# A new written-out order for a sketched attention with an MLP: loads on two queues, batch-0 queries loaded by head pairs

## The chip, the core and the metric

The kernel runs on one core of a Trainium2 chip. The core has five engines that work side by side, each with its own queue of instructions in a fixed order: TensorE (PE, matmuls; its weight loads are listed as PEld), VectorE (DVE), ScalarE (ACT), GpSimd (POOL) and SyncE (SP, which here only issues DMAs). An instruction that waits holds back everything behind it on its engine. The metric is the device time of one execution in microseconds (us), median of three runs.

## The reference

Two blocks follow each other. The first is an attention with a polynomial sketch, for batch 4, heads 4, sequence 1088 and head size 32, with r = 8:

```
a = S1 x,  b = S2 x                      # 8 numbers each, for x = q and x = k
phi(x) = a outer b                       # 64 features per token
kv = sum over tokens of phi(k) v         # 64 x 32 per head
z  = sum over tokens of phi(k)           # 64 per head
attn = phi(q) kv / (phi(q) z + 1e-6)
```

The heads are then laid side by side to rows x of 128 numbers, and the second block is

```
xn  = (x - mean) / sqrt(var + 1e-6) * g
out = x + relu(xn w_ch1) w_ch2           # w_ch1 128 x 512, w_ch2 512 x 128
```

q, k, v and g are float32; S1, S2, w_ch1 and w_ch2 are float64 and are turned into float32 on the chip with integer and float steps on their two 32-bit words.

## The kernel before, in words

All work is written as small named operations, and one long string, PROGRAM (from line 851), lists them in the order in which they are issued; an operation's first argument is often the engine (S SyncE, A ScalarE, V VectorE, G GpSimd). Each engine's queue is that list, filtered to the engine. No scheduler changes it.

For a batch b, the steps are: load k (ld, 544 KB, all 1088 tokens; batch 0 in two pieces), transpose it on VectorE (turn_g, turn_r, lines 427 and 437), make the features a and b (k_dir with its copy k_cp for batch 0, line 462; k_feat and k_tok for the others, lines 480 and 489), multiply them out into kp (k_prod, line 87, on GpSimd or VectorE), sum them for the denominator (k_sum, line 504, k_zs, k_sc, k_sccp) and multiply them with v (k_val, line 541). Queries go the same way: turned, q_dir (batch 0, line 576) or q_feat and q_tok (lines 614 and 623), then q_ac, q_den, q_rec (denominator), q_a2, q_prod (line 87), q_turn (line 661), and num (line 675) multiplies them with kv. num_cp copies the result into xT. Each batch gives two chunks of 512 rows, and pairs of batches share a chunk for the 64 remaining tokens: chunks 0 to 9.

For each chunk, hid (line 784) multiplies with w_ch1, relu (lines 792, 794) follows, sec (line 800) multiplies with w_ch2; row_turn, row_wr and row_rd bring x back to rows by way of a DRAM buffer, st_bn, st_ag and st_pow make the row's 1/sqrt(var), and fin or fin_a with fin_g write the result, which store sends out. Before hid, w_ch1 is folded with g and the mean (c_cg, fold, fold_cp). fill is a matmul of ones that nobody reads; there are seven of them.

Batch 0's queries are an exception in how they are loaded: ld_t and ld_tr put them into qt, and TensorE turns them (turn_p, turn_c). One ld_t of before brings half of the columns of all four heads, in runs of 512 bytes.

Loads go through eight completion semaphores, DMAHW0 to DMAHW7, which are handed out in turn over all DMAs of SyncE and ScalarE together. A DMA that takes a semaphore which an earlier DMA has used waits, in its issuing engine's queue, until that earlier one has landed. In the rows below, the first DMAHW number behind a DMA is the one that it takes.

## Time and profile before

| | |
|---|---|
| runs | 108.47, 104.01 and 107.0 us, median 107.0 |
| the profiled execution | 104.49 us, of which 102.7 us is the span of the trace |
| TensorE busy | 94.6 us (92% of the span), granted clock 1.0 throughout |
| VectorE, GpSimd, ScalarE busy | 70.8, 63.1, 39.6 us |
| DMA | 14.37 MB, mean 140 GB/s |

The trace's times start with the span. The chain of waits is the work that ended last, followed back from the end. A row of the timeline reads: start, duration, engine, line, operation, what it writes and reads, count. A row of windows gives the busy time of each engine in a stretch, the clock, the share of the 16 DMA engines that was busy (as packets overlap a little it can pass 1) and what they moved.

### The profile page before, as it was taken

The numbers are of one execution on the slowest core, as the hardware profiler recorded it, in microseconds if no ns is written. First come the engines' busy times: TensorE is split into PE (matmuls) and PEld (weight loads), VectorE is DVE, ScalarE is ACT, GpSimd is POOL, SyncE is SP. The second block draws the span as 40 slices with busy tenths as digits, with TensorE's granted clock in tenths as the row PEclk, the third lists the DMA queues.
The fourth block names the chain that finished last, engine by engine and source line by source line (L and its number), as shares of the span: only waits on it lengthen the run. The fifth ranks groups of instructions, "written<-read, shape, count | busy, mean of one in ns | idle before, by whom it ended". The sixth has DMA issues, their size and how long they took to land.

```text
span 102.7 us, 3149 instructions
## 1 busy us (share of the span) xinstructions
PE 94.6 (92%) x1269; PEld 68.2 (66%) x1269; DVE 70.8 (69%) x216; ACT 39.6 (39%) x99; POOL 63.1 (61%) x88
## 2 busy tenths in 40 slices
PE   5936899999999999999999999999999999999950
...
GB/s 68 193 319 396 277 203 241 274 244 123 311 182 150 156 190 20 6 57 158 160 152 6 0 109 177 231 102 0 6 105 115 123 200 203 1 102 6 0 147 83
DMA packets 13567, 14.37 MB, mean 140 GB/s; under 512 B 2416, under 2 KB 10096, under 8 KB 13552
## 3 DMA queue, kind: packets, MB, share of 16 engines
...
q10 hardware_dynamic: 112, 0.04, 0.2%
q14 instruction: 5, 0.04, 0.1%
q0 software_dynamic: 32, 0.00, 0.0%
HBM read 9.84 MB, written 4.33 MB: 138 GB/s over the span
## 4 chain that ended last, share of the span: by engine, by line
PE 71%; POOL 12%; DVE 6%; DMA 5%; issue 1%; SPq 1%; ACT 0%; DVEq 0%
PE ALL L800 31%; PE ALL L784 25%; DMA w_raw<-in_moe_w_ch_dram 5%; PE ALL L675 4%; PE ALL L541 3%; POOL qp L87 2%; POOL kp L87 2%; POOL mant L318 2%; POOL cg L350 2%; PE ALL L614 1%; POOL w L87 1%; PE ALL L576 1%; DVE kf L489 1%; PE ALL L249 1%; POOL ac L87 1%
## 5 line engine op out<-in xcount | busy, mean ns | idle before, releaser
L800 PEld LDWEIGHTS ALL<-w,hT 128*128 128x128 f32 x272 | 32.6, 192 | 6.1 <-issue 3.6
L800 PE MATMUL ALL<-w,hT 128*128 128x128 f32 x272 | 34.4, 277 | 0.1
L784 PE MATMUL ALL<-xT,w 128*128 128x512 f32 (+1 forms) x72 | 30.0, 548 | 0.0
L792 ACT ACTIVATE hT<-ALL 128x512 f32<-128x512 f32 (+2 forms) x35 | 15.9, 485 | 25.5 <-PE ALL L784 21.3
L87 POOL TENSOR_TENSOR qp<-a,fq 128x512 f32<-128x512 f32 (+3 forms) x10 | 17.7, 1780 | 1.6 <-DVE a L87 1.4
L784 PEld LDWEIGHTS ALL<-xT,w 128*128 128x128 f32 x72 | 12.4, 190 | 8.3 <-issue 5.3
L87 POOL TENSOR_TENSOR kp<-kf 128x1280 f32<-128x1280 f32 (+2 forms) x6 | 12.5, 2096 | 0.0
L770 POOL TENSOR_TENSOR rstd<-va,mhalf 128x4 f32<-128x4 f32 (+1 forms) x10 | 9.2, 922 | 3.0 <-ACT ob L818 2.3
L661 DVE STREAM_TRANSPOSE qpT<-qp 128x1280 f32<-128x1280 f32 (+2 forms) x9 | 10.9, 1219 | 0.0
L813 DVE SCALAR_TENSOR_TENSOR ob<-ALL,rstd,x 128x128 f32<-128x128 f32 x12 | 4.1, 348 | 9.6 <-PE ALL L800 7.4
L818 ACT ACTIVATE ob<-ALL,rstd 128x128 f32<-128x128 f32 x20 | 6.7, 368 | 9.9 <-PE ALL L800 5.1
L794 DVE TENSOR_SCALAR hT<-ALL 128x512 f32<-128x512 f32 (+1 forms) x9 | 5.7, 635 | 5.2 <-PE ALL L784 2.9
L737 DVE STREAM_TRANSPOSE xh<-ALL 128x256 f32<-128x256 f32 x16 | 6.5, 422 | 3.3 <-ACT ob L818 2.5
L82 ACT COPY xT<-ALL 128x256 f32<-128x256 f32 x11 | 6.9, 643 | 4.3 <-PE ALL L675 3.0
L828 POOL TENSOR_TENSOR ob<-ob,x 128x512 f32<-128x512 f32 x4 | 5.1, 1283 | 5.5 <-ACT ob L818 5.5
L768 POOL TENSOR_TENSOR va<-mv,eps 128x4 f32<-128x4 f32 (+1 forms) x10 | 2.0, 197 | 10.3 <-DVE mv L763 10.2
L249 PE MATMUL ALL<-ones 128*128 128x512 f32 (+1 forms) x14 | 7.3, 636 | 1.0 <-DVE m L197 1.0
L675 PE MATMUL ALL<-qpT,kvr 32*32 32x288 f32 (+2 forms) x320 | 7.5, 363 | 0.1
L757 DVE BATCH_NORM_STATS2 st<-x 128x6 f32<-128x128 f32 x32 | 6.7, 274 | 0.0
L675 PEld LDWEIGHTS ALL<-qpT,kvr 32*32 32x32 f32 x320 | 4.4, 103 | 2.7 <-issue 1.3
L541 PEld LDWEIGHTS ALL<-kp,vn 128*32 128x32 f32 x288 | 4.2, 110 | 2.2 <-ACT hT L792 0.8
L87 POOL TENSOR_TENSOR ac<-fq 128x160 f32<-128x160 f32 (+1 forms) x7 | 3.6, 508 | 2.3 <-ACT qT L82 1.8
...
## 6 DMA issues: line engine op xcount, KB each, us to landing
...
xd<-xh SPq DMA_DIRECT2D x8, 256.0 KB, 2.4
x<-xd SPq DMA_DIRECT2D x8, 256.0 KB, 2.8
out_dram<-ob SPq DMA_DIRECT2D x7, 256.0 KB, 2.7
...
qt<-in_q_dram SPq DMA_DIRECT2D x2, 256.0 KB, 2.7
w_raw<-in_moe_w_ch_dram SPq DMA_DIRECT2D x2, 256.0 KB, 5.0
```

Source lines behind the costliest of these rows:

```text
L82: act.copy(o, i)
L87: by[eng].tensor_tensor(out=o, in0=a, in1=b, op=ALU.mult)
L249: pe.matmul(bank(z, 0, w), ones, _ap(ones, 0, P, 0, [[0, w // P], [1, P]]), start=True, stop=True)
L541: pe.matmul(bank(z, 0, F)[D * h : D * h + D], vn[b][:, TW * h + D * u : TW * h + D * (u + 1)], kp[:, H * F * u + F * h : H * F * u + F * ( ...
L661: dve.transpose(_ap(qpT, 0, P, 32 * u0, [[32, u1 - u0], [TW, 8], [1, 32]]), qp[:, H * F * u0 : H * F * u1])
L675: pe.matmul(bank(z[r], o, o + w)[D * h : D * h + D], kvr[b % 2][rows, DM * f + D * h : DM * f + D * h + D], qpT[rows, c : c + w], start=(f ...
L757: dve.bn_stats(out=sts[slot(c)][:, 6 * t : 6 * t + 6], in_=row_ap(c, t))
L770: pool.tensor_tensor(out=rstds[slot(c)][:, 0:n], in0=vas[slot(c)][:, 0:n], in1=mhalf[:, 0:n], op=ALU.pow)
L784: pe.matmul(bank(z, 0, n), w1[:, P * j : P * (j + 1)], cols(c)[:, a : a + n], start=True, stop=True)
L792: act.activation(o, i, AF.Relu)
L800: pe.matmul(bank(z, DM * t, DM * (t + 1)), h[:, 512 * j + P * t : 512 * j + P * (t + 1)], w2[:, DM * j : DM * (j + 1)], start=(j == 0), st ...
L818: act.activation(ob(c)[:, P * t : P * (t + 1)], bank(z, P * t, P * (t + 1)), AF.Copy, scale=rstds[slot(c)][:, t : t + 1])
```

## The change

Three operations change: the load of g can be issued from any engine; ld_t brings two whole heads in runs of 1 KB, instead of half of the columns of four heads in runs of 512 bytes; and PROGRAM is a new order of the same operations, with other engines for some and other PSUM banks. Loads that stood on SyncE's queue alone (but for S1, S2 and the last store) are now spread over SyncE's and ScalarE's queues: SyncE issues 51 DMAs instead of 66, ScalarE 19 instead of 3, GpSimd none instead of one. The number of matmuls, fills among them, is the same. GpSimd gives six tensor-tensor operations to VectorE, and takes from it the clearing of ones and two steps of the conversion of w_ch1 and w_ch2.

```
     @op
-    def ld_g():
-        pool.dma_start(out=g_raw, in_=moe_g_ln.rearrange("(p o) -> p o", o=1))
+    def ld_g(eng):
+        by[eng].dma_start(out=g_raw, in_=moe_g_ln.rearrange("(p o) -> p o", o=1))
...
-    def ld_t(eng, u0, u1):
+    def ld_t(eng, h0, h1):
         by[eng].dma_start(
-            out=_ap(qt, 0, P, D * u0, [[8 * D, H], [1, D * (u1 - u0)]]),
-            in_=bass.AP(q.tensor, q.offset + u0 * D,
-                        [[8 * D, P], [S * D, H], [1, D * (u1 - u0)]]),
+            out=_ap(qt, 0, P, 8 * D * h0, [[8 * D, h1 - h0], [1, 8 * D]]),
+            in_=bass.AP(q.tensor, q.offset + h0 * S * D,
+                        [[8 * D, P], [S * D, h1 - h0], [1, 8 * D]]),
         )
...
-    ld_t S 0 4; ld_s A 1; ld_g; c_ones V; c_small; ld_w S 1 2 4; ld_s A 0; c_ac 1; ld_w S 1 0 2;
...
+    ld_w S 1 2 4; c_ones G; c_small; c_ac 1; c_act; fill 1 512 6; ld_vr S 3 0; c_ident; c_vpad 0;
...
```

ScalarE, from the start of its queue. In before, after the loads of S1 and S2, its rows are conversions of w_ch1 (low, exf, mant), the copy of turned queries (qT) and k_cp, the copies into kf; "waits" names the semaphores that a row waits for (PE, DVE: that engine's own).

```order
L112 DMA s_raw_66<-in_S2_dram 8x32
L112 DMA s_raw_66<-in_S1_dram 8x32
L201 ACT_TABLE_LOAD
L201 ACTIVATE warm_89<-one_80 128x1 [waits DVE_49]
L304 ACTIVATE low1_116<-w1_raw_77 128x256 [waits DMAHW3_49]
L288 ACTIVATE exf1_114<-ex1_113,m896_88 128x256 [waits DVE_49]
L82 COPY qT0_97<-ALL_65 128x512 [waits PE_49]
L296 ACTIVATE mant1_115<-bits1_112,one_80 128x256 [waits DVE_49]
L304 ACTIVATE low1_116<-w1_raw_77 128x256 [waits DMAHW4_49]
L82 COPY kf0_130<-ALL_65 128x192 [waits PE_49]
```

In the changed kernel, the same place of ScalarE's queue, from the two loads of batch 0's k (kn0) to k_cp:

```order
L121 DMA kn0_68<-in_k_dram 128x512
L304 ACTIVATE low1_116<-w1_raw_77 128x256 [waits DMAHW0_49]
L296 ACTIVATE mant1_115<-bits1_112,one_80 128x256 [waits DVE_49]
L129 DMA vn0_73<-in_v_dram 32x4x256 [waits DMAHW4_49]
L116 DMA g_raw_67<-in_moe_g_ln_dram 128x1 [waits DMAHW6_49]
L414 COPY skq1_102<-ALL_65 128x16 [waits PE_49]
L304 ACTIVATE low1_116<-w1_raw_77 128x256 [waits DMAHW7_49]
L143 DMA qt_70<-in_q_dram 128x2x256 [waits DMAHW0_49]
L288 ACTIVATE exf1_114<-ex1_113,m896_88 128x256 [waits DVE_49]
L151 DMA qt_70<-in_q_dram 64x4x32 [waits DMAHW2_49]
L82 COPY s2c_106<-ALL_65 128x128 [waits DVE_49]
L121 DMA kn0_68<-in_k_dram 128x1088 [waits DMAHW4_49,DMAHW3_49,DVE_49]
```

k_cp comes right behind that last row. So five loads moved ahead of k_cp on ScalarE, and each takes a semaphore that an earlier DMA holds. SyncE's first rows in the changed kernel tell which:

```order
L159 DMA w1_raw_77<-in_moe_w_ch1_dram 128x256
L135 DMA vn3_76<-in_v_dram 32x4x32
L112 DMA s_raw_66<-in_S1_dram 8x32
L112 DMA s_raw_66<-in_S2_dram 8x32
L143 DMA qt_70<-in_q_dram 128x2x256
L159 DMA w1_raw_77<-in_moe_w_ch1_dram 128x256
L161 DMA w2_raw_78<-in_moe_w_ch2_dram 128x2x256 [waits DMAHW0_49]
L121 DMA kn1_69<-in_k_dram 128x1088 [waits DMAHW1_49]
L129 DMA vn0_73<-in_v_dram 32x4x256 [waits DMAHW2_49]
```

w_ch2's load (w2_raw, 512 KB) holds DMAHW0, for which ScalarE's row L143 waits; a quarter of batch 0's v (vn0, 128 KB) holds DMAHW2, for which ScalarE's row L151 waits; the second piece of kn0 holds DMAHW6, for which the load of g waits. In before, w2_raw stood behind the two pieces of kn0 on SyncE, and no load stood on ScalarE behind the table load.

VectorE, around the first hid. In before, behind the two copies of batch 1's q features (L623) and q_turn (L661) of batch 0 come transposes of loaded keys and queries (L427, L437), the turns of chunk 1's rows (L737) and q_den, q_rec, and then the product kp of batch 1 (L87, kp_132):

```order
L737 STREAM_TRANSPOSE xh0_158<-ALL_65 128x256 x2
L623 STREAM_TRANSPOSE fq_137<-ALL_65 128x2x9x32 x2
L661 STREAM_TRANSPOSE qpT_139<-qp_138 128x5x8x32
L427 STREAM_TRANSPOSE kT1_96<-kn1_69 128x4x8x32
L437 STREAM_TRANSPOSE kT1_96<-kn1_69 128x64
```

In the changed kernel:

```order
L84 COPY xT0_146<-ALL_65 128x2x128
L737 STREAM_TRANSPOSE xh0_158<-ALL_65 128x256 x2
L623 STREAM_TRANSPOSE fq_137<-ALL_65 128x2x9x32 x2
L661 STREAM_TRANSPOSE qpT_139<-qp_138 128x5x8x32
L794 TENSOR_SCALAR hT0_183<-ALL_65 128x256
L87 TENSOR_TENSOR kp_132<-kf1_131 128x1280
```

A relu and five of the nine ninths of kp of batch 1 now stand right behind q_turn; a copy into xT stands ahead.

TensorE, at the same place. In before, k_sum (L504) and k_sc (L518) of batch 2 stand ahead of the first hid (L784), and a whole chunk's hid and 8 sec (L800) between the second num (L675) and k_val of batch 1 (L541):

```order
L504 MATMUL ALL_65<-kf0_130 32x32 x9
L675 MATMUL ALL_65<-qpT_139,kvr0_135 32x128 x32
L518 MATMUL ALL_65<-zT_133,s2b_129 128x32
L249 MATMUL ALL_65<-ones_79 128x256
L614 MATMUL ALL_65<-qT1_98,skq1_102 32x288 x16
L784 MATMUL ALL_65<-xT0_146,w1_123 128x256 x8
L675 MATMUL ALL_65<-qpT_139,kvr0_135 32x160 x32
L480 MATMUL ALL_65<-kT1_96,sk8_128 32x288 x8
L800 MATMUL ALL_65<-w2_124,hT0_183 128x128 x8
L784 MATMUL ALL_65<-xT1_147,w1_123 128x512 x4
L541 MATMUL ALL_65<-kp_132,vn1_74 32x64 x36
```

In the changed kernel:

```order
L675 MATMUL ALL_65<-qpT_139,kvr0_135 32x128 x32
L614 MATMUL ALL_65<-qT1_98,skq1_102 32x288 x16
L784 MATMUL ALL_65<-xT0_146,w1_123 128x256 x8
L675 MATMUL ALL_65<-qpT_139,kvr0_135 32x160 x32
L541 MATMUL ALL_65<-kp_132,vn1_74 32x64 x36
L784 MATMUL ALL_65<-xT1_147,w1_123 128x512 x4
```

k_val of batch 1 moved up to right behind the second num, and k_sum and k_sc of batch 2 moved to behind it.

165 lines of the change are left out of this document (82 added, 83 removed).

## The prediction

> **What bounds the kernel now.** I read the page first, then the chain of waits, then TensorE's timeline for the places where the matmuls change kind.
>
> ```profile
> PE 94.6 (92%) x1269; PEld 68.2 (66%) x1269; DVE 70.8 (69%) x216; ACT 39.6 (39%) x99; POOL 63.1 (61%) x88
> PE   5936899999999999999999999999999999999950
> 40.00:50.00 10.00, 10.00 (x185) 7.63 (x184) 7.21 (x28) 4.18 (x11) 8.45 (x11) 1.00 0.22 71
> 94.46 4.48 PE ALL L800 x40
> 98.97 0.35 DVE ob L813
> ```
>
> From about 15 us to the last sec at 98.94 (94.46 + 4.48) TensorE is full, and the chain runs along it. Behind it lie one fin (0.35) and the last store, to 102.7. So the time is three things: when the chain of batch 0 reaches the first hid, how much matmul work is left then, and the holes after it. The number of matmuls does not change.
>
> ```profile
> 10.16 2.12 PE L462 MATMUL ALL<-sk,kT 128*128 128x64 f32 x18
> 13.34 0.39 PE L504 MATMUL ALL<-kf 128*32 128x32 f32 x18
> 15.39 1.10 PE L576 MATMUL ALL<-skd,qT 128*128 128x96 f32 x8
> 22.28 1.06 PE L675 MATMUL ALL<-qpT,kvr 32*32 32x128 f32 x64
> 23.27 0.41 PE L518 MATMUL ALL<-zT,s2b 128*128 128x32 f32 x2
> 24.82 3.72 PE L784 MATMUL ALL<-xT,w 128*128 128x256 f32 x16
> 28.48 1.48 PE L675 MATMUL ALL<-qpT,kvr 32*32 32x160 f32 x64
> 29.89 0.71 PE L480 MATMUL ALL<-kT,sk 64*32 64x288 f32 x16
> ```
>
> The stations of batch 0: k_dir at 10.16, k_sum at 13.34, q_dir at 15.39, num at 22.28, the first hid at 24.82. Before k_dir, TensorE has almost only fills; the loads set that time:
>
> ```profile
> 3.00:4.00 1.00, 1.00 (x5) 0.66 (x4) 0.90 (x6) 0.20 (x1) 0.88 (x5) 1.00 0.69 201
> 4.00:5.00 1.00, 1.00 (x5) 0.78 (x4) 0.39 (x5) 0.00 (x0) 0.00 (x0) 1.00 0.56 110
> 5.00:6.00 1.00, 1.00 (x4) 0.38 (x2) 0.04 (x1) 0.05 (x1) 0.00 (x0) 1.00 0.83 273
> 8.00:10.00 2.00, 1.36 (x6) 0.85 (x7) 1.97 (x8) 1.15 (x3) 1.88 (x3) 1.00 1.05 404
> 10.00:12.00 2.00, 2.00 (x18) 1.99 (x18) 2.00 (x7) 1.02 (x4) 2.00 (x8) 1.00 0.94 241
> ```
>
> The last two columns are the busy share of the 16 DMA engines and GB/s. From 8 to 12 us they are full with one issuing queue. Between 3 and 6 us they move much less.
>
> **Loads on two queues.** The engines are full while SyncE alone feeds them, so a second queue cannot make the same bytes arrive sooner; it changes who stands ahead of whom. The Trainium skill says the same (DMA: Bandwidth & Descriptors, Issuing engines are not separate DMA queues: all queues end at the same 16 engines, and only issuing time is saved); by that rule the change gains nothing from the spread, and the share of 1.05 agrees.
>
> ```profile
> 2.27 0.91 SPq L121 DMA_DIRECT2D kn<-in_k_dram  x2
> 3.22 0.43 SPq L161 DMA_DIRECT2D w_raw<-in_moe_w_ch_dram  x1
> 4.21 0.76 SPq L151 DMA_DIRECT2D qt<-in_q_dram  x1
> 10.22 0.33 SPq L121 DMA_DIRECT2D kn<-in_k_dram  x1
> w_raw<-in_moe_w_ch_dram SPq DMA_DIRECT2D x1, 512.0 KB, 6.6
> kn<-in_k_dram SPq DMA_DIRECT2D x1, 256.0 KB, 5.7
> 10.98 0.32 ACT L82 COPY kf<-ALL 128x192 f32<-128x192 f32 x1 [1.83 <-PE ALL L462]
> 11.88 0.75 ACT L82 COPY kf<-ALL 128x192 f32<-128x192 f32 x2
> 12.53 0.27 ACT L82 COPY s2c<-ALL 128x128 f32<-128x128 f32 x1
> ```
>
> What matters is ScalarE's queue, where k_cp, the copies that k_sum needs, now stand behind five loads. The load of half the queries waits for the semaphore of w_ch2's load. That one landed at 3.22 + 6.6 = 9.8, with 1824 KB issued up to and with it. In the changed kernel 1844 KB are issued up to it, and up to 128 KB of v besides on the other queue: 20 to 148 KB, at 404 GB/s up to 0.4 us; I take 10.0. Next ScalarE issues the remaining queries, which wait for a quarter of v that stands behind batch 1's k on SyncE: 544 + 128 KB = 688 kB, 1.7 us at 404 GB/s, 2.9 us at 241. I take 2.0, nearer the stretch with long runs, as these bytes are: 12.0. Then 0.76 for that issue, 0.27 for the copy s2c, 0.33 for one more k load, 13.4; then three copies, the first 0.32 and the other two 0.75 to the end: 14.4 against 11.88 + 0.75 = 12.6 now. k_sum follows at 14.4, not 13.34.
>
> k_dir itself hardly moves: the second piece of k, the latter of the two issued from 2.27 on, landed at about 2.7 + 5.7 = 8.4; behind it the load of g is issued now, then a short copy, then VectorE's mask and a transpose, some 1.5 us, again about 10. Should k come 2 us sooner it would not help, since k_cp waits for 13.4 anyway. (The skill's rule in Queues, rings and completion order, that each engine serves its queues in turn packet by packet, puts k half a queue ahead of the queries and w_ch1 beside it. No row here shows two full queues.) The 1 KB runs save issue time or nothing: the 512-byte halves are not late now.
>
> ```profile
> 11.43 0.94 DVE L87 TENSOR_TENSOR kp<-ALL,kf 128x768 f32<-128x768 f32 x1
> 14.96 0.29 DVE L524 TENSOR_TENSOR skd<-ALL,m 128x128 f32<-128x128 f32 x1 [0.49 <-PE ALL L518]
> 16.42 1.20 DVE L427 STREAM_TRANSPOSE kT<-kn 128x1024 f32<-128x1024 f32 x1
> 18.03 0.21 DVE L643 RECIPROCAL rden<-den 128x16 f32<-128x16 f32 x1
> 18.80 1.07 POOL L87 TENSOR_TENSOR qp<-a,fq 128x512 f32<-128x512 f32 x1
> 21.42 0.71 DVE L661 STREAM_TRANSPOSE qpT<-qp 128x512 f32<-128x512 f32 x1
> ```
>
> **From k_cp to the first hid.** VectorE: the first copy is there at 13.7, a product 0.94, two small ones to 15.2, zT, the second product to 16.2, k_sccp 0.29: q_dir at 16.5, which is 1.1 late. Then two transposes of 1.20 and k_sccr between stand ahead of q_den: 19.0. q_den 0.30 and q_rec 0.21, 19.5; on GpSimd q_a2 0.4, a product 1.07, q_ac 0.5, a product 1.07: 22.5; q_turn 0.71: 23.2; num 1.06, copies into xT 0.6 with their latencies: hid at 25.2. In before, num started at 22.28 but k_sc, a fill and q_feat stood between it and hid, of which only q_feat is left. **First term: 25.2 − 24.82 = +0.4.**
>
> **Work left.** Batch 2's k_sum and k_sc, done by 24.82 now, come after hid: 0.33 for L504 (from the chain below) and 23.51 − 23.27 = 0.24 for L518, where the fill at 23.51 begins. As TensorE is full afterwards they count in full. **Second term: +0.55.**
>
> ```profile
> 21.90 0.33 PE ALL L504 x18
> 23.51 0.68 PE L249 MATMUL ALL<-ones 128*128 128x256 f32 x2
> 25.49 1.45 DVE L623 STREAM_TRANSPOSE fq<-ALL 128x576 f32<-128x576 f32 x2 [0.45 <-POOL qp L87]
> 26.87 1.47 DVE L661 STREAM_TRANSPOSE qpT<-qp 128x1280 f32<-128x1280 f32 x1
> 33.51 1.73 DVE L87 TENSOR_TENSOR kp<-kf 128x1024 f32<-128x1024 f32 x1
> L737 DVE STREAM_TRANSPOSE xh<-ALL 128x256 f32<-128x256 f32 x16 | 6.5, 422 | 3.3 <-ACT ob L818 2.5
> ```
>
> **The hole.** k_val of batch 1 stands right behind the second num, and needs a product of 1280 elements that VectorE now makes. From hid on VectorE has two row_turns (0.8), two q_tok (1.45), q_turn (1.47), a relu of 256 columns (0.4, an estimate), and the product, 1.73 × 1280/1024 = 2.2: 6.3, less some 0.07 where each overlaps the next, 5.9. TensorE has hid, 28.48 − 24.82 = 3.66, and num, 29.89 − 28.48 = 1.41: 5.1. So it waits 0.8. If rows of DVE overlap more, 0.4; if q_tok starts late behind GpSimd as at 25.49 (0.45 of idle), 1.2. **Third term: +0.8.**
>
> **What costs nothing.** g off GpSimd: its issue lay in GpSimd's idle start, and c_cg is needed before fold only, which comes after q_dir now. S1 and S2 behind w_ch1 on SyncE: their conversion ends by 8 us, before k. The conversion of w_ch2, spread over GpSimd and VectorE: it must end before the first sec, and a chunk's hid (3.7 us) lies between; without that cover it would cost up to 1 us. GpSimd's products given to VectorE later: both have room (70.8 and 63.1 of 102.7). From 40 us on, TensorE is busy throughout (10.00 of 10 in the window quoted first), and I see no second place of the kind of the hole. The end is the same sec, fin and store.
>
> Sum: 0.4 + 0.55 + 0.8 = +1.75, say +1.8 on the profiled 104.49: 106.3. That execution is near the low end of what is known of this kernel (108.47, 104.01, 107.0, and 104.49); the median of the three runs stands 2.5 above it. What lies between is not in this trace, so I leave it in both kernels and put the term on the median: 107.0 + 1.8 = **108.8 us**, 1.7% more. Two per cent of 107.0 is 2.1 us, about what a measurement here can tell from no change; so within 2% means 104.9 to 109.1.
>
> **Rivals.**
>
> *Slower: ScalarE stuck behind its loads for longer.* If the quarter of v lands not at 12.0 but at 13.2, because batch 1's k, v and half of the queries (256 KB more) share the engines at 241 GB/s ((688 + 262) kB / 241 = 3.9 instead of 2.0 us, less half as the queries end last), everything behind is 1.2 later: +3.0, which is 110.0. It decides from 12.5 us on. For it: 241 GB/s in the very stretch. Against: those bytes were in short runs.
>
> *Faster: the poor start goes.* Between 3 and 6 us the engines moved (404 − 201) + (404 − 110) + (404 − 273) = 628 kB less than at full rate, 1.6 us. If that came from one queue standing behind a slow load of w_ch1, or from g's load through GpSimd, all landings come 1.6 earlier and the sum is +0.2. If it is also why before's runs differ by 4.5 us, the changed kernel's runs stay together at about 104.49 + 0.2 = 104.7, 2.1% under 107.0. It decides from w_ch1's first half landing before 3.5 us. For it: g's load took 5.0 us in that time:
>
> ```profile
> g_raw<-in_moe_g_ln_dram POOLq DMA_DIRECT2D x1, 0.5 KB, 5.0
> ```
>
> Against: w_ch1's load still comes first, on its own.
>
> *It does nothing.* VectorE starts its product sooner than I sum, and the start's delay is eaten by the fill that no longer stands ahead of hid: 107.0.
>
> **How the numbers follow.** Forecast 0.43, its own range 107.9 to 109.1 (the hole from 0.4 to 1.2, and half a microsecond for the start, give 107.9 to 109.6; what lies above 109.1 is counted with the slower rival). Nothing 0.10, also within 2%. Slower rival 0.30. Faster rival 0.17. So faster 0.17, same 0.53, slower 0.30. The range leaves out a tenth at each end: from 104.5, just under the faster rival, to 110.6, above the slower one.
>
> **What would show it.** ScalarE idle from about 9.5 to 13.4 us and ended by DMAs, k_cp's copies from 13.4, k_sum at 14.4, q_dir at 16.5, hid at 25.2, a wait of L541 for kp of VectorE of 0.8 near 30, and the last sec ending at 100.7. It is wrong if k_cp starts before 12.5, if L541 does not wait, or if TensorE has holes after 40 us.

## The result and the profile after

The changed kernel takes 111.9 us (median of four executions: 111.0, 111.5, 112.3 and 113.5), the kernel before 105.5 (median of 103.3, 104.0, 107.0 and 108.5). The ratio is 1.077, with a 95% interval of 1.065 to 1.089; it leaves out executions that lie more than 1.5% above the fastest of the same kernel. The forecast was 108.8 us, with a range to 110.6: the time lies above the range, on the side of the slower rival and beyond it.

The profiled execution is the one of 113.5 us, with a span of 111.7. From its page, busy time of TensorE, its busy share and its granted clock in 40 slices of the span, and the shares of the chain that ended last:

```profile
PE 101.3 (91%) x1269; PEld 72.9 (65%) x1269; DVE 77.0 (69%) x223; ACT 37.7 (34%) x95; POOL 58.6 (52%) x84
...
PE   6859829999999999599999999999999999999970
...
PEclk9985996555999999999999999999999999999999
...
PE 71%; DMA 21%; DVE 4%; issue 1%; DVEq 0%
```

The number of matmuls is the same (1269), yet TensorE is busy 101.3 us instead of 94.6: its clock fell to half within slices 3 to 4 and 7 to 10. The chain passes through DMAs for 21% of the span; in before it was 5%. Its timeline at the stations that the prediction followed (start, duration; in brackets the idle time ahead and what ended it):

```profile
6.82 0.36 PE L370 MATMUL ALL<-ident,s_f 16*128 16x16 f32 x2 [1.57 <-DVE s_f L87]
...
10.07 2.43 PE L462 MATMUL ALL<-sk,kT 128*128 128x64 f32 x18
...
15.22 0.71 PE L504 MATMUL ALL<-kf 128*32 128x32 f32 x18 [1.81 <-ACT kf L82]
16.95 0.66 PE L445 MATMUL ALL<-ident,qt 128*128 128x128 f32 x4 [1.02 <-DMA qt<-in_q_dram]
...
18.97 1.86 PE L576 MATMUL ALL<-skd,qT 128*128 128x96 f32 x8
...
29.57 0.96 PE L675 MATMUL ALL<-qpT,kvr 32*32 32x128 f32 x57
...
31.81 3.69 PE L784 MATMUL ALL<-xT,w 128*128 128x256 f32 x16 [0.16 <-DVE xh L737]
35.43 1.17 PE L675 MATMUL ALL<-qpT,kvr 32*32 32x160 f32 x64
36.54 1.21 PE L541 MATMUL ALL<-kp,vn 128*32 128x64 f32 x72
...
46.72 0.41 PE L518 MATMUL ALL<-zT,s2b 128*128 128x32 f32 x2 [1.29 <-DVE zT L512]
...
106.21 1.95 PE L800 MATMUL ALL<-w,hT 128*128 128x128 f32 x16
```

k_dir stands where it stood (10.07, before 10.16). k_sum is 1.9 late, q_dir 3.6, and its eight matmuls take 1.86 instead of 1.10. num starts at 29.57 (before 22.28) and the first hid at 31.81 (before 24.82). The last sec ends at 106.21 + 1.95 = 108.16 (before 98.94). So of the 9.2 us, 7.0 are lost ahead of the first hid and 76.35 − 74.12 = 2.2 behind it, 1.29 of which is one hole that ends at 46.72. Ahead of hid it is the clock that shows and not waits: from 17.5 to 27.8 us TensorE is busy almost throughout at half clock. From k_sum to hid it took 16.59 us; it was 11.48 in before, and the forecast had 10.8.

ScalarE and its DMA issues (ACTq) in the same execution:

```profile
5.23 0.34 ACTq L129 DMA_DIRECT2D vn<-in_v_dram  x1
5.61 0.51 ACTq L116 DMA_DIRECT2D g_raw<-in_moe_g_ln_dram  x1
...
9.53 0.39 ACTq L143 DMA_DIRECT2D qt<-in_q_dram  x1
...
13.43 0.73 ACTq L151 DMA_DIRECT2D qt<-in_q_dram  x1
14.21 0.27 ACT L82 COPY s2c<-ALL 128x128 f32<-128x128 f32 x1 [3.73 <-DMA vn<-in_v_dram]
14.31 0.50 ACTq L121 DMA_DIRECT2D kn<-in_k_dram  x1
14.85 0.32 ACT L82 COPY kf<-ALL 128x192 f32<-128x192 f32 x1 [0.38 <-issue]
```

ScalarE does no work for 3.73 us, from 10.48 to 14.21. Until 13.43 (2.95 us) it stands for the landing of v's quarter, whose semaphore the load of the remaining queries needs; the rest is mostly the issue of that load (0.73). k_cp starts at 14.85.

### The profile page after: what moved, and what is told of

Its sections match the earlier page's. It is cut to its first block, busy times and chain, and to the rows that moved or that the text cites. A ratio compares the mean times of both kernels' runs of the same rounds, so it can differ in the third digit from the quotient of the medians.

```text
span 111.7 us, 3151 instructions
## 1 busy us (share of the span) xinstructions
PE 101.3 (91%) x1269; PEld 72.9 (65%) x1269; DVE 77.0 (69%) x223; ACT 37.7 (34%) x95; POOL 58.6 (52%) x84
## 4 chain that ended last, share of the span: by engine, by line
PE 71%; DMA 21%; DVE 4%; issue 1%; DVEq 0%
PE ALL L800 26%; PE ALL L784 24%; DMA w_raw<-in_moe_w_ch_dram 8%; DMA qt<-in_q_dram 7%; PE ALL L675 5%; DMA x<-xd 4%; PE ALL L541 4%; PE ALL L576 4%; DMA xd<-xh 3%; PE ALL L480 2%; PE ALL L445 2%; PE ALL L518 1%; PE ALL L614 1%; PE ALL L355 1%; DVE xT L84 1%; DVE xh L737 1%
## 5 line engine op out<-in xcount | busy, mean ns | idle before, releaser
L800 PEld LDWEIGHTS ALL<-w,hT 128*128 128x128 f32 x272 | 32.7, 192 | 5.2 <-issue 3.8
L800 PE MATMUL ALL<-w,hT 128*128 128x128 f32 x272 | 34.3, 278 | 0.0
L784 PE MATMUL ALL<-xT,w 128*128 128x512 f32 (+1 forms) x72 | 30.5, 552 | 0.2 <-DVE xh L737 0.2
L792 ACT ACTIVATE hT<-ALL 128x512 f32<-128x512 f32 (+2 forms) x31 | 14.5, 502 | 24.4 <-PE ALL L784 18.2
L784 PEld LDWEIGHTS ALL<-xT,w 128*128 128x128 f32 x72 | 12.5, 190 | 8.4 <-issue 5.5
L87 POOL TENSOR_TENSOR qp<-a,fq 128x512 f32<-128x512 f32 (+3 forms) x9 | 15.3, 1706 | 3.4 <-DVE a L87 3.1
L768 POOL TENSOR_TENSOR va<-mv,eps 128x4 f32<-128x4 f32 (+1 forms) x10 | 3.1, 313 | 20.4 <-DVE mv L763 20.4
L794 DVE TENSOR_SCALAR hT<-ALL 128x512 f32<-128x512 f32 (+2 forms) x13 | 7.3, 567 | 6.2 <-PE ALL L784 3.2
L661 DVE STREAM_TRANSPOSE qpT<-qp 128x1280 f32<-128x1280 f32 (+2 forms) x9 | 10.9, 1219 | 0.9 <-POOL qp L87 0.8
L87 POOL TENSOR_TENSOR kp<-kf 128x1024 f32<-128x1024 f32 (+2 forms) x5 | 10.2, 2032 | 1.6 <-ACT kf L82 1.6
L249 PE MATMUL ALL<-ones 128*128 128x512 f32 (+1 forms) x14 | 8.3, 738 | 1.0 <-POOL ones L192 1.0
L308 POOL TENSOR_SCALAR ex<-exf 128x256 uint32<-128x256 f32 (+1 forms) x3 | 4.3, 1421 | 7.0 <-ACT exf L288 4.7
L675 PE MATMUL ALL<-qpT,kvr 32*32 32x288 f32 (+2 forms) x320 | 7.0, 364 | 0.0
L737 DVE STREAM_TRANSPOSE xh<-ALL 128x256 f32<-128x256 f32 x16 | 6.1, 421 | 1.1 <-PE ALL L675 1.1
L87 POOL TENSOR_TENSOR ac<-fq 128x128 f32<-128x128 f32 (+1 forms) x6 | 3.7, 624 | 5.2 <-ACT fq L82 3.9
L249 PEld LDWEIGHTS ALL<-ones 128*128 128x128 f32 x14 | 3.5, 273 | 3.9 <-issue 2.8
L541 PEld LDWEIGHTS ALL<-kp,vn 128*32 128x32 f32 x288 | 5.1, 126 | 1.2 <-POOL ac L87 0.9
```

What stands on the lines that cost most here:

```text
L87: by[eng].tensor_tensor(out=o, in0=a, in1=b, op=ALU.mult)
L249: pe.matmul(bank(z, 0, w), ones, _ap(ones, 0, P, 0, [[0, w // P], [1, P]]), start=True, stop=True)
L541: pe.matmul(bank(z, 0, F)[D * h : D * h + D], vn[b][:, TW * h + D * u : TW * h + D * (u + 1)], kp[:, H * F * u + F * h : H * F * u + F * ( ...
L661: dve.transpose(_ap(qpT, 0, P, 32 * u0, [[32, u1 - u0], [TW, 8], [1, 32]]), qp[:, H * F * u0 : H * F * u1])
L675: pe.matmul(bank(z[r], o, o + w)[D * h : D * h + D], kvr[b % 2][rows, DM * f + D * h : DM * f + D * h + D], qpT[rows, c : c + w], start=(f ...
L737: dve.transpose(_ap(xh[slot(c)], 0, P, 64 * n * i, [[32 * n, 2], [32, n], [1, 32]]), pair(z, P * (c % 2), [[32, n], [1, 32]]))
```

## The experiments

Times are in us, with the mean granted clock of that execution in brackets; a profile is the first execution of its kernel.

### What the clock has to do with it

**The kernel before, again.** No edit.

> The kernel before, unchanged, for the granted clock of each of its executions. Its four known times lie between 103.3 and 108.5 us. Clock theory: TensorE's granted clock is decided in steps of 3.41 us that do not start with the kernel (in the changed kernel's profile it falls at 7.3, rises at 10.7, falls at 17.5 and rises at 27.8, all whole multiples of 3.41 apart), so before too has executions with half clock, and these are the slow ones: 103 to 104.5 us at a clock of 1.00, 106 to 108.5 at 0.95 to 0.98. Rival (waits and DMA): the clock is 1.00 in all executions and the 5 us of spread come from elsewhere.

Eight of twelve executions took 103.3 to 104.4 (0.992 to 1.000), four 106.7 to 108.8 (0.952 to 0.967), and none lay between. The 17 executions of before that ran beside these kernels divide in the same way, and one at 0.739 took 127.9; in a later set of 16, two did lie between (105.8 at 0.984, 106.3 at 0.976). The profiled one is among the four (108.21). Windows cut at the steps of its clock, with the busy time of TensorE in the second column and the granted clock third from the end:

```profile
5.20:8.60 3.40, 1.43 (x6) 0.61 (x5) 1.77 (x8) 1.44 (x4) 0.83 (x1) 1.00 0.99 328
8.60:12.00 3.40, 3.40 (x11) 2.30 (x11) 2.63 (x9) 0.28 (x1) 3.32 (x10) 0.50 0.98 320
12.00:15.40 3.40, 3.40 (x17) 3.24 (x16) 2.47 (x3) 1.68 (x6) 0.62 (x3) 0.50 0.88 250
15.40:18.80 3.40, 3.40 (x26) 1.81 (x25) 0.55 (x4) 1.31 (x4) 2.07 (x4) 0.50 0.74 212
18.80:22.20 3.40, 3.40 (x39) 2.68 (x37) 3.34 (x10) 1.18 (x3) 1.24 (x3) 1.00 0.28 47
```

After a step in which TensorE was busy 1.43 of 3.41 us the clock was half for three steps; hid came at 28.59 instead of 24.82, and the last sec 3.7 later than in the profile at full clock. So the spread of before's times is in the main its clock, and the 107.0 on which the forecast was built was in all likelihood an execution at half clock (its clock is not on record).

**The changed kernel with more fills.**

```
-    fill 1 256 6; fill 1 256 1; sk 7;
+    fill 1 256 6; fill 1 256 1; fill 1 512 1; sk 7;
...
-    fill 1 512 0; k_prod0 0 3 5 0;
+    fill 3 512 0; k_prod0 0 3 5 0;
...
-    turn_p 0 0 4;
+    fill 1 256 1; turn_p 0 0 4;
```

> The changed kernel with four more fills (matmuls nobody reads, 1.46 us for 512 columns at full clock): 512 columns ahead of TensorE's wait for s_f at 5.25 us, 1024 behind k_dir at 13.4, 256 behind k_sum at 15.9. No real work is moved. Clock theory: the mean clock rises from 0.94 to 0.97 to 0.99 or 1.00; k_sum and the turns of the queries stay at 15.2 and about 17, but q_dir to num shrinks from 10.6 us towards the 6.9 of before: num near 26, last sec near 104.5, time 107.5 to 108.5 us, 3 to 4 below the changed kernel. Rival (the waits alone): fills cannot make a load land sooner; k_sum 15.2, num 29, 111 to 112 us as now.

109.9 (0.993), 110.2 (1.000), 111.1 (0.969), 112.0 (0.985). At full clock that is 1.2 below the mean of the changed kernel's two executions at 0.969 (111.25): a third of what the clock theory expected. (The fill's price was put too high: in the traces 512 columns take 0.93 to 0.97 us at full clock, and 1.45 is the price of 768.) In the profile the clock is 1.00 until 26.5, q_dir's matmuls take 1.10 again, and another wait has come out, in the middle of k_val:

```profile
22.63 1.06 PE L541 MATMUL ALL<-kp,vn 128*32 128x64 f32 x61
25.45 0.32 PE L541 MATMUL ALL<-kp,vn 128*32 128x64 f32 x8 [1.76 <-DMA vn<-in_v_dram]
```

The last eight matmuls of k_val stand for a piece of v. At half clock k_val came to them late enough not to see it: the clock had hidden it. From k_sum to hid this profile, at full clock almost throughout, still takes 15.59 us.

**The kernel before with more fills**, in three sizes, where its TensorE waits 2.61 us for s_f. The edit of the middle one:

```
-    fill 1 512 1; fill 1 256 7; w_mant V 1 256 512;
+    fill 1 512 1; fill 1 256 7; fill 1 512 1; fill 1 256 7; w_mant V 1 256 512;
```

> The kernel before with 1280 more columns of fill (about 2.4 us at full clock) where its TensorE waits 2.61 us for s_f, at 6.03; nothing else. Clock theory: the executions of before at 0.944 to 0.968 (106.5 to 108.8 us, about half of them) are those in which the 3.41 us step fell on that idle time; with it filled they go, nearly all executions lie at 103.3 to 104.5, and the median over all falls from about 106 to 103.7. Rival (the half clock comes from elsewhere, or from chance): as many executions above 106 as in before.

> The kernel before with 768 more columns of fill (1.45 us) in its idle time before s_f, where 1280 gave 103.8 to 104.9 with no execution of low clock, but ended 0.8 us after s_f was there. Theory: sk comes when s_f does, the clock still holds: all executions at 103.2 to 104.3, median 103.7. Rival: the 0.8 to 1.2 us of idle left are enough for the step to fall: some executions at 106 to 108.5.

> The kernel before with only 512 more columns of fill (0.97 us) in its idle time of 2.61 us before s_f; 768 and 1280 columns took every execution of low clock away. Theory (the step looks at how much of its 3.41 us TensorE was busy): with 1.6 us idle left, as much as the idle time at which the changed kernel's clock falls in some executions, some executions still lie at 106 to 108.5, fewer than in before (where half do); those at full clock at 103.1 to 104.0. Rival (any idle time below 2.4 us is safe in this place): none above 105.

| more fill, columns | executions | lowest clock | times | median |
|---|---|---|---|---|
| none (c1_before) | 12 | 0.952 | 103.3 to 108.8 | 104.3 |
| 512 | 12 | 0.978 | 103.2 to 105.2 | 104.0 |
| 768 | 12 | 0.992 | 103.6 to 104.6 | 104.3 |
| 1280 | 12 | 0.992 | 103.8 to 104.9 | 104.5 |

One execution of 36 still lost clock (0.978, 105.2), with the smallest fill. Before, beside the fill of 768 on the same chip, had a median of 107.0 over 19 executions, 11 of them above 106. At full clock on both sides the fill of 768 costs 0.5% (ratio 1.005, interval 1.002 to 1.008), that of 512 nothing that can be measured (1.002, 0.997 to 1.007). What the fill buys is that before's executions at low clock no longer come up. Against before's best executions, at full clock, it gains nothing.

### What the loads have to do with it

**Four loads off ScalarE ahead of k_cp.**

```
-    ld_w S 1 0 2; ld_w S 2 0 4;
+    ld_w S 1 0 2; ld_t S 0 2; ld_tr S; ld_w S 2 0 4; ld_g S;
...
-    fill 1 256 5; ld_g A; sk_q 7;
+    fill 1 256 5; sk_q 7;
...
-    ld_t A 0 2; w_ex V 1 0 256;
+    w_ex V 1 0 256;
...
-    sk_d 7; ld_tr A;
+    sk_d 7;
...
-    turn_r k 0; ld A k 2 0 34;
+    turn_r k 0;
...
-    k_cp A 0 6 9 4; sk_d4 A;
+    k_cp A 0 6 9 4; ld A k 2 0 34; sk_d4 A;
```

> The changed kernel with four of the five loads off ScalarE's queue ahead of k_cp: the other half of the queries, the remaining queries and g are issued by SyncE ahead of w_ch2 and behind it, batch 2's k by ScalarE right behind k_cp. Waits theory: k_cp no longer stands behind the landing of v at 14.2; it follows k_dir, at about 12.3, k_sum at 12.8 to 13.3, q_dir at 15.5 to 16.5 provided the queries land by 14; hid 5 to 6 us sooner, time 105 to 107 us. Clock theory: the same only as far as the clock comes back with it; if TensorE's clock still falls near 17 us, 108 to 110. If ScalarE's loads are not the cause, 111 to 112.

109.7 (0.984), 110.7 (0.953), 112.6 (0.969), 114.8 (0.950): little or no gain. The first half of the theory held: k_sum at 13.18, q_dir at 16.38, no wait for the queries. Then the next landings hold it, first batch 2's k on VectorE, ahead of batch 1's features, then v:

```profile
20.71 1.25 DVE L427 STREAM_TRANSPOSE kT<-kn 128x1024 f32<-128x1024 f32 x1 [3.25 <-DMA kn<-in_k_dram]
```

```profile
23.12 0.53 PE L504 MATMUL ALL<-kf 128*32 128x32 f32 x18 [3.05 <-DVE kf L489]
...
26.25 0.44 PE L541 MATMUL ALL<-kp,vn 128*32 128x64 f32 x8 [0.88 <-DMA vn<-in_v_dram]
```

The idle time made the clock fall besides (half from 23.1 to 33.3), and hid came at 32.46.

**v's last two pieces earlier**, on top of the fills.

```
-    ld_v S 0 0; ld_vr S 0 1;
+    ld_v S 0 0; ld_vr S 0 1; ld_vr S 0 0; ld_v S 0 2;
...
-    turn_c A 0 0 4; ld_v A 0 2;
+    turn_c A 0 0 4;
...
-    ld_vr A 1 1; ld_vr A 0 0;
+    ld_vr A 1 1;
```

> The kernel with four more fills, and the last two pieces of batch 0's v (128 KB and 16 KB) that ScalarE issued behind the copies of the queries issued by SyncE right behind the first pieces, ahead of batch 1's queries. With the fills alone TensorE waits 1.76 us for v in the middle of k_val, at 25.45. Theory: that wait is only the landing of these pieces; it goes, hid comes 1.5 to 1.8 us sooner (29), 108.3 to 108.7 us where the fills alone gave 109.9 to 110.2 at full clock. Rival (the 16 DMA engines are full until 22 us, so what is moved ahead pushes back the rest): the queries and k land later, and k_sum or q_dir lose what k_val gains: 109.5 to 110.5.

109.1, 109.7, 110.1 (all 0.999 or 1.000) and 113.1 (0.948). k_val no longer waits, and in the profile hid comes at 27.82, 13.36 us behind k_sum; but the times at full clock are only some 0.4 below those with the fills alone. That is the rival's size.

**One queue instead of two.** The twelve loads of ScalarE ahead of the first hid are written with S instead of A, at the same places; three of them:

```
-    ld A k 0 16 34; ld_t S 2 4; ld A k 0 0 16;
+    ld S k 0 16 34; ld_t S 2 4; ld S k 0 0 16;
...
-    turn_r k 0; ld A k 2 0 34;
+    turn_r k 0; ld S k 2 0 34;
```

> The changed kernel with the twelve loads that ScalarE issues ahead of the first hid issued by SyncE at the same places of the written order: the spread over two queues taken back, the order of the loads kept. Theory 1 (ScalarE's queue is the harm): k_cp follows k_dir, k_sum at 13 to 14; but k0 is issued 1 to 2 us later, k_val still waits for v's last piece, which stands far back in the one queue: hid 28 to 30, 107.5 to 109.5. Theory 2 (the order of the loads is the harm, the queue incidental): v's last piece and the queries land as late as now, hid 30 to 32, 110 to 112. Theory 3 (the second queue helps): 112 to 114.

108.7 and 110.1 (0.968), 110.1 (0.953), 110.0 (0.932): 1.9 less than the changed kernel at the same clock (0.968 against 0.969: 109.4 against 111.25). All four lie below all four of the changed kernel, and hid came at 29.82. So the second queue costs rather than helps, and most of the loss stays without it. The size lies between the two theories.

**Before's order of loads under the changed order of work.**

```
-    ld_w S 1 2 4; c_ones G; c_small; c_ac 1; c_act; fill 1 512 6; ld_vr S 3 0; c_ident; c_vpad 0;
+    ld_t S 0 2; ld_s A 1; ld_w S 1 2 4; ld_s A 0; c_ones G; c_small; c_ac 1; c_act; ld_w S 1 0 2;
+    ld_g A; ld S k 0 16 34; ld S k 0 0 16; ld_w S 2 0 4; ld S k 1 0 34; ld_tr S; ld_t S 2 4;
...
-    turn_r k 0; ld A k 2 0 34;
+    turn_r k 0; ld S k 2 0 34; ld_vr S 1 1; ld_vr S 0 0; ld_vr S 2 1; ld_v S 0 3; ld_v S 0 2;
+    ld_vr S 1 0; ld_v S 0 1; ld_v S 0 0; ld_v S 1 3; ld_vr S 0 1; ld S q 1 0 34;
```

> The changed kernel with its order of work on TensorE, VectorE, GpSimd and ScalarE's copies kept, but every load ahead of the first hid issued in the order of before, from SyncE (S1, S2 and g from ScalarE, ahead of any copy); the queries stay in head pairs. Loads theory (the 6 to 7 us lost ahead of hid come from which load lands when: v's quarter and the queries holding ScalarE, v's last piece holding k_val): k_sum near 13.5, q_dir near 16, no wait of k_val for v, hid at 25 to 26.5; with the 0.55 of deferred work and the hole of 1.3 before 46.7 still in it, 105 to 106.5 us at full clock, 1 to 3% above before. Rival (the new order of work on VectorE and GpSimd): hid still at 30 or later, 109 to 111. If TensorE's clock falls during it, 2 to 4 us more.

106.0 (0.978), 108.7 (0.984), 110.1 (0.968), 112.5 (0.963). The first, profiled, shows the changed order of work without late landings ahead of hid:

```profile
13.30 0.38 PE L504 MATMUL ALL<-kf 128*32 128x32 f32 x18
...
15.99 1.10 PE L576 MATMUL ALL<-skd,qT 128*128 128x96 f32 x8 [0.27 <-DVE skd L524]
...
19.86 1.21 PE L541 MATMUL ALL<-kp,vn 128*32 128x64 f32 x72
...
25.09 3.69 PE L784 MATMUL ALL<-xT,w 128*128 128x256 f32 x16 [0.28 <-DVE xh L737]
28.71 1.18 PE L675 MATMUL ALL<-qpT,kvr 32*32 32x160 f32 x64
30.63 1.21 PE L541 MATMUL ALL<-kp,vn 128*32 128x64 f32 x72 [0.75 <-ACT xT L82]
...
98.66 1.95 PE L800 MATMUL ALL<-w,hT 128*128 128x128 f32 x16
```

hid at 25.09, where the prediction had 25.2, and the last sec ends at 100.61, where it had 100.7. That is partly luck. No load stands in ScalarE's queue here, so k_sum stood at 13.30 and not at the 14.4 of the sum; from k_sum to hid it took 11.79 us, where the sum had 10.8 and before took 11.48. The other three executions are not explained by their clock alone.

The trace puts L541's 0.75 down to ScalarE's copy into xT, which k_val does not read. What it reads and what came last is a quarter of batch 1's v: issued at 25.68, landed 4.8 us later, at 30.5.

**The same, with a fill ahead of s_f.**

```
-    fill 1 256 6; fill 1 256 1; sk 7;
+    fill 1 256 6; fill 1 256 1; fill 1 512 1; sk 7;
```

> The changed kernel's order of work with before's order of loads, as in the run before it, and one more fill of 512 columns (0.97 us at full clock) where TensorE waited 1.38 us for s_f at 5.4. In that run one profile had hid at 25.1 and last sec at 100.6 (106.0 us, clock 0.978), the other executions 108.7 to 112.5 at 0.963 to 0.984. Clock theory: with the idle time filled the clock stays at 0.99 or more in all executions and they draw together at 105.3 to 106.0: what the order of work alone costs against before at full clock (103.7) is then 1.6 to 2.3 us. Rival: the spread is of the loads' landings, not of the clock: executions still between 106 and 112 at a clock near 1.

107.0 (1.000), 107.2 (0.977), 109.2 (0.984), 111.2 (0.969): the clock theory explains it in part only. In its profile VectorE stood 1.76 us for batch 0's k and 1.59 for batch 1's queries, for which it had not waited above. The landings themselves differ between executions; why, these runs don't tell.

**Columns instead of head pairs**, in the changed kernel, with ld_t as it was in before:

```
-    ld A k 0 16 34; ld_t S 2 4;
+    ld A k 0 16 34; ld_t S 0 4;
...
-    w_low A 1 0 256; ld_t A 0 2;
+    w_low A 1 0 256; ld_t A 4 8;
```

> The changed kernel with batch 0's queries loaded as before, half of the columns of all four heads in runs of 512 bytes, from the same two places (SyncE, then ScalarE); nothing else undone. The first turns of queries then need only the load that SyncE issues at 2.4 us. Theory (head pairs made the first turns wait for ScalarE's load): the wait of 1.0 us for the queries ahead of L445 goes; but k_sum still comes at 15.2 and zT, VectorE's work and v's last piece stand as they do, so q_dir gains at most 0.5: 110.5 to 111.5. Rival (the queries' wait is on the path in full): 110.0 or less. Rival (runs of 512 bytes cost the engines): slower than 111.5.

111.5 to 112.1 (0.946 to 0.969): no difference. The wait of L445 for the queries is gone, but k_sc then waits 1.31 for zT, and q_dir comes at 18.31.

And head pairs alone in before, with ld_t as it is in the changed kernel:

```
-    ld_t S 0 4; ld_s A 1;
+    ld_t S 0 2; ld_s A 1;
...
-    fill 1 256 6; ld_tr S; w_ex V 1 256 512;
+    fill 1 256 6; ld_t S 2 4; ld_tr S; w_ex V 1 256 512;
...
-    ld_t S 4 8; w_e2 V 0 0 32;
+    w_e2 V 0 0 32;
```

> The kernel before with one part of the change alone: ld_t brings two whole heads in runs of 1 KB instead of half of the columns of four heads in 512 bytes; since turn_p of the first half of the columns needs all four heads, both loads now stand ahead of it, the second ahead of the remaining queries on SyncE. Theory: 256 KB more ahead of TensorE's first turns and of the copy on ScalarE behind them, both with room until 12 us; batch 1's k lands before it as now: 103.3 to 104.5 at full clock, no difference. Rival (head pairs themselves cost): TensorE stands at turn_p until the second load has landed, near 9 to 10 us, sk, k_dir behind it come 1 to 2 us later, and 105 to 106 at full clock.

109.8 (1.000), 110.9 (0.969), 115.8 (0.994), 115.9 (0.995). Here head pairs cost 6 us or more, since before turns its queries first of all:

```profile
11.27 0.69 PE L445 MATMUL ALL<-ident,qt 128*128 128x128 f32 x2 [6.79 <-DMA qt<-in_q_dram]
```

TensorE stands 6.79 us for the second pair, and sk and k_dir wait behind it: the rival's mechanism at several times its size.

### The hole behind 40 us

In the changed kernel VectorE does chunk 1's st_bn ahead of zT of batch 2, and waits there for the rows.

```
-    st_bn 0; turn_r k 3; st_ag 0; q_rec 1 4 9; st_bn 1; st_ag 1;
+    st_bn 0; turn_r k 3; st_ag 0; q_rec 1 4 9;
...
-    k_zs 2 4; k_tok 3 0 1;
+    k_zs 2 4; k_tok 3 0 1; st_bn 1; st_ag 1;
```

> The changed kernel with chunk 1's st_bn and st_ag moved on VectorE from ahead of zT of batch 2 (k_zs) to behind k_tok of batch 3, nothing else. In the changed kernel's profile VectorE waits 1.95 us for chunk 1's rows (the DMA x<-xd) at 43.5 to 45.4, and TensorE 1.29 us for zT before L518 at 46.7. Theory: that hole goes, 1.2 to 1.3 us less: 110.0 to 110.6 us against 111.3 to 111.9. Rival: the work that follows (products on GpSimd behind st_pow, num of batch 1) is late anyway and the hole moves there: less than 0.4 us.

110.0 (0.965), 110.9 (0.969), 111.7 (0.953), 112.4 (0.954). In the profile of the changed kernel that wait is

```profile
45.44 0.87 DVE L757 BATCH_NORM_STATS2 st<-x 128x6 f32<-128x128 f32 x4 [1.95 <-DMA x<-xd]
```

With the edit L518 no longer waits, and from hid to the last sec's end the profile has 105.47 − 30.49 = 74.98 instead of 76.35. In time that is 0.4 at 0.969 and nothing at 0.954; with four executions it is not separated from nothing. Nor is it shown that the place of st_bn decides: L518's wait is missing also in profiles in which st_bn stayed where it was (more fills, v's pieces earlier, one queue, and both with before's loads), and there in others (1.19 with four loads off ScalarE, 1.01 with columns). It takes rows that land late as well.

### Taking the landings away one by one

Each of these goes on from the last.

**Three causes together:** the queries, g and batch 2's k as in "four loads off ScalarE", all of batch 0's v ahead of batch 1's queries, one fill of 512 ahead of s_f. On top of "four loads off ScalarE":

```
-    fill 1 256 6; fill 1 256 1; sk 7;
+    fill 1 256 6; fill 1 256 1; fill 1 512 1; sk 7;
...
-    ld_v S 0 0; ld_vr S 0 1;
+    ld_v S 0 0; ld_vr S 0 1; ld_vr S 0 0; ld_v S 0 2; ld_v S 0 3;
...
-    sk_qq 3; ld S q 1 0 34;
+    sk_qq 3;
...
-    turn_c A 0 0 4; ld_v A 0 2; turn_p 1 4 8; ld_v S 0 3;
+    turn_c A 0 0 4; turn_p 1 4 8;
...
-    ld_vr S 2 1;
+    ld_vr S 2 1; ld S q 1 0 34;
...
-    ld_vr A 1 1; ld_vr A 0 0;
+    ld_vr A 1 1;
```

> The changed kernel with the three delays seen so far taken away together and two queues kept: the other half of the queries, the remaining queries and g on SyncE early, batch 2's k on ScalarE behind k_cp, all pieces of batch 0's v on SyncE ahead of batch 1's queries, which go behind q_dir; one more fill of 512 ahead of s_f. Theory (three causes add up: ScalarE held by a landing, v's tail, the clock): k_sum 13.2, q_dir 16.4, no wait of k_val, hid 25 to 27, 105 to 107 us. Rival (whatever is moved ahead delays something else, because the engines are full until 22 us): batch 2's k lands at 20 or later, VectorE stands at its transpose ahead of k_tok of batch 1 as before, hid 28 or later, 108 to 110.

106.3 (0.993), 107.5 and 107.7 (0.984, 0.983), 108.1 (0.961). hid at 27.01, and k_sum late at 14.60: the last part of k_dir stood 1.56 us for a transpose on VectorE that is behind w_ch2's conversion, which waited 2.08 for its load.

```profile
12.08 0.50 DVE L277 TENSOR_SCALAR ex<-w_raw 128x512 uint32<-128x512 uint32 x1 [2.08 <-DMA w_raw<-in_moe_w_ch_dram]
```

**That conversion and the queries' transpose behind other work:**

```
-    sk_c A 7; w_ex V 2 0 512; turn_r k 0;
+    sk_c A 7; turn_r k 0;
...
-    w_bits V 2 0 512; w_mant V 2 0 512; w_mant V 1 0 256;
+    w_mant V 1 0 256;
...
-    k_sccr 0 6;
+    k_sccr 0 6; w_ex V 2 0 512; w_bits V 2 0 512; w_mant V 2 0 512;
...
-    q_prod G 0 2 4; turn_g q 1 0 4;
+    q_prod G 0 2 4;
...
-    q_turn 0 2;
+    q_turn 0 2; turn_g q 1 0 4;
```

> The run with the three causes taken away, and two steps of VectorE that wait for loads moved behind work that does not: the first steps of w_ch2's conversion from ahead of k0's last transpose (2.08 us of waiting for w_ch2 there) to behind k_sccr, and the transpose of batch 1's queries (0.70 us of waiting, 1.59 in another run) from ahead of k_zs of batch 1 to behind q_turn. Theory (the new order puts work that waits for late loads ahead of the chain of batch 0, with no room for a landing that comes 1 to 2 us late): k_sum at 12.5 to 13, q_dir at 15.5 to 16, hid at 24.5 to 25.5, 104.5 to 105.5 us, within 1.5% of before at full clock. Rival (the order behind hid costs the rest): hid comes that early but last sec stays 76 us behind it, 106 to 107.

108.1 to 110.7 (0.962 to 0.969), well above what was expected. k_sum comes at 12.32, as expected; then zT waits behind a transpose that stands 2.93 us for batch 1's k, TensorE 2.85 for zT, and the clock falls.

```profile
15.09 0.24 DVE L437 STREAM_TRANSPOSE kT<-kn 128x64 f32<-128x64 f32 x1 [2.93 <-DMA kn<-in_k_dram]
```

**Batch 1's k loaded earlier, its last transpose later:**

```
-    ld_t S 0 2; ld_tr S; ld_w S 2 0 4;
+    ld_t S 0 2; ld S k 1 0 34; ld_tr S; ld_w S 2 0 4;
...
-    turn_g k 0 2 4; ld S k 1 0 34;
+    turn_g k 0 2 4;
...
-    k_sum 0 6; turn_r k 1;
+    k_sum 0 6;
...
-    k_sccr 0 6;
+    k_sccr 0 6; turn_r k 1;
```

> As the run before it (the three causes away, w_ch2's conversion and the queries' transpose moved back), and batch 1's k, on whose landing at 15.1 VectorE stood 2.93 us ahead of zT there: its load goes ahead of w_ch2's on SyncE, its last transpose behind k_sccr. Theory (each landing stands ahead of the chain of batch 0, one behind the other; with this one out of the way none is left ahead of q_dir): zT right behind k_sum, q_dir at 15.5 to 16.3, hid at 24.5 to 26, 104.8 to 106.5 us. Rival (the changed order always finds another landing, since the bytes ahead of 22 us are the same): hid at 27 or later, 107.5 or more.

107.3 and 107.9 (1.000), 109.7 (0.968), 110.3 (0.966), again above the range. zT is prompt, and now ScalarE's queue holds q_dir: batch 2's k, issued there, needs the semaphore that w_ch2's load still has, and the copies of the queries stand behind it.

```profile
14.67 0.35 ACTq L121 DMA_DIRECT2D kn<-in_k_dram  x1
15.06 0.41 ACT L82 COPY skd<-skd 128x256 f32<-128x256 f32 x1 [3.40 <-DVE kT L427]
```

```profile
16.18 1.79 PE L576 MATMUL ALL<-skd,qT 128*128 128x96 f32 x8 [2.46 <-ACT qT L82]
```

The trace puts ScalarE's 3.40 down to a transpose that had ended at 9.9; they end when that issue goes out. The next run bears this out: with that load and three more off ScalarE's queue, q_dir came at 14.05.

**Four more loads ahead of hid from ScalarE to SyncE** (`ld A k 2 0 34`, `ld_v A 1 2`, `ld_vr A 1 1` and `ld_v A 1 3`, of which the first:)

```
-    k_cp A 0 6 9 4; ld A k 2 0 34;
+    k_cp A 0 6 9 4; ld S k 2 0 34;
```

> As the run before it, in which TensorE stood 2.46 us ahead of q_dir for ScalarE's copy of the queries, and ScalarE 3.40 us ahead of that behind its issue of batch 2's k, whose semaphore (DMAHW3) w_ch2's load still held: the four loads that ScalarE still issues between k_cp and the first hid go to SyncE. Theory (a load in ScalarE's queue, held by its semaphore, holds the copies behind it): q_dir at 13.8 to 14.5, no wait of it for ScalarE, hid at 23.5 to 25.5, and with no idle time above 1 us ahead of it the clock holds at 0.99 or more: 103.8 to 105.5 us. Rival (another landing takes its place): VectorE stands for batch 2's k or batch 1's queries, hid at 26.5 or later, 106.5 or more.

107.9 and 108.5 (0.984), 110.2 and 110.3 (0.969), above the range. q_dir at 14.05, earlier than in before (15.39). Then VectorE stands for batch 2's k:

```profile
19.02 1.25 DVE L427 STREAM_TRANSPOSE kT<-kn 128x1024 f32<-128x1024 f32 x1 [2.63 <-DMA kn<-in_k_dram]
```

**That transpose later, g earlier:**

```
-    ld_w S 2 0 4; ld_g S;
+    ld_g S; ld_w S 2 0 4;
...
-    k_sccr 0 6; turn_r k 1; w_ex V 2 0 512; w_bits V 2 0 512; w_mant V 2 0 512; turn_g k 2 0 4;
+    k_sccr 0 6; turn_r k 1; w_ex V 2 0 512; w_bits V 2 0 512; w_mant V 2 0 512;
...
-    turn_r k 2; k_zs 1 1; q_prod G 0 0 2; q_den 0 4 9;
+    k_zs 1 1; q_prod G 0 0 2; q_den 0 4 9; turn_g k 2 0 4; turn_r k 2;
```

> As the run before it, in which TensorE stood 2.24 us for batch 1's k features (L489 on VectorE), behind a transpose of batch 2's k that waited 2.63 us for its load, and 1.17 us for g: that transpose goes behind q_den of batch 0, and the load of g ahead of w_ch2's. Theory (with the last landing out of the way the changed order of work is as good as the sum of the prediction made it): hid at 24 to 25.5, clock 0.99 or more, 104 to 105.8 us. Rival (v's pieces or batch 2's k hold k_val or q_turn next): hid at 26.5 or later, 106.5 or more.

106.4, 106.6, 106.9 (1.000) and 107.6 (0.999), a ratio of 1.026 to before (1.018 to 1.035): for the first time all executions of a changed kernel are at full clock and close together, though above the range expected. hid is at 26.41 (expected by 25.5), and the last sec ends at 102.17, 3.2 later than in before: 1.6 are lost ahead of hid and 1.6 behind it (75.76 against 74.12):

```profile
18.73 0.38 PE L504 MATMUL ALL<-kf 128*32 128x32 f32 x18 [0.85 <-DVE kf L489]
...
22.54 0.72 PE L480 MATMUL ALL<-kT,sk 64*32 64x288 f32 x16 [1.18 <-DVE skq L528]
...
26.41 3.69 PE L784 MATMUL ALL<-xT,w 128*128 128x256 f32 x16
```

Neither wait shown is for a load. L504 waits for a transpose that stands behind the moved conversion of w_ch2 on VectorE (15.31 to 17.54). L528 stands behind the moved transpose of batch 2's k (20.46 to 21.70), ahead of which VectorE waited 0.78 for GpSimd.

## Why the prediction was wrong

**ScalarE behind its loads: the mechanism right, the landing too early.** The step "I take 2.0 ...: 12.0" failed. The remaining queries went out at 13.43, close to the slower rival's 13.2, and k_cp started at 14.85. k_sum then stood at 15.22 instead of 14.4. The load ahead was not late: w_ch2 had landed by 9.53, where the sum had 10.0. The size that was wrong is the 2.0 us behind it, which measured 3.9 (9.53 to 13.43), the engines moving 236 GB/s. That is the slower rival's 3.9 before it takes anything off; "less half", by its own numbers, gives some 13, and its 13.2 does not follow exactly. The prediction had quoted 241 GB/s for the very stretch; the changed kernel moved 239 in its windows of 10.7 to 14.1 and of 14.1 to 17.5. "Against: those bytes were in short runs" was no reason.

**"The 1 KB runs save issue time or nothing"** held for the time (columns instead: 111.5 to 112.1), though the wait for the second pair is there (1.02).

**From k_cp to the first hid: the step that failed most.** The first term, +0.4, measured +6.99 (hid at 31.81); the three together, +1.75, measured +9.22. The step summed the work of the engines, took every load behind the quarter of v as landed in time, and put the clock at nothing. In the changed kernel's own profile the loss shows as half clock: from 17.5 to 27.8 us TensorE is busy 10.24 us with about 5.1 us of work. Once fills keep the clock up, the waits come out instead, and k_sum to hid still takes 15.59 us.

In the kernels changed further, v's last piece (1.76, TensorE), batch 2's k (3.25 and 2.63, VectorE), w_ch2 (2.08, VectorE), batch 1's k (2.93, VectorE) and a load held in ScalarE's queue (3.40) stood ahead of the chain of batch 0, one after the other, as soon as the one ahead of them was gone. Each of these waits is shown in a run; none is worth its length alone, as the next one takes its place: taking four loads off ScalarE gained nothing sure, v's last pieces 0.4. How the 7.0 divide between clock and landings stays open. With before's order of loads hid came at 25.09 for 25.2 in one execution, but by luck in part: k_sum was 1.1 earlier than the sum had it, and the engines' work from there, with the loads in time, was 1.0 longer than it says.

**Spread over two queues.** "A second queue cannot make the same bytes arrive sooner" agrees with what was measured: up to 12 us the engines moved 244 GB/s in the changed kernel and 242 in before. It cost 1.9 us. The Trainium skill (DMA: Bandwidth & Descriptors, Issuing engines are not separate DMA queues) has it that the spread gains little more than issuing time; the runs agree that there is no gain, and the page does not give the cost.

**The clock was not in the prediction.** Its page of before showed 1.00, and the text read no more from it. Windows of the changed kernel, cut at its clock's steps, columns as above:

```profile
3.90:7.30 3.40, 1.83 (x10) 1.17 (x8) 2.60 (x13) 0.73 (x2) 1.10 (x1) 1.00 0.93 271
7.30:10.70 3.40, 3.40 (x10) 2.15 (x9) 3.11 (x12) 1.01 (x3) 0.14 (x1) 0.50 1.04 313
10.70:14.10 3.40, 2.71 (x18) 1.88 (x17) 0.58 (x2) 0.00 (x0) 2.79 (x13) 1.00 1.05 239
14.10:17.50 3.40, 1.26 (x22) 0.87 (x22) 2.30 (x4) 1.33 (x5) 1.82 (x3) 1.00 1.02 239
17.50:20.90 3.40, 3.37 (x16) 3.10 (x15) 3.40 (x6) 1.20 (x3) 1.25 (x2) 0.51 0.71 167
20.90:24.40 3.50, 3.50 (x27) 2.47 (x28) 2.57 (x6) 0.56 (x2) 2.60 (x4) 0.50 0.52 167
24.40:27.80 3.40, 3.40 (x94) 2.64 (x93) 1.07 (x4) 1.24 (x3) 1.55 (x2) 0.50 0.01 3
```

Two steps with TensorE busy 1.83 and 1.26 us are each followed by half clock, the second for three steps. Every execution of the changed kernel had some (0.939 to 0.969), as its waits of 1 to 2 us leave such steps wherever the steps fall; before's one wait of 2.61 did so in about half of its executions. At full clock the changed kernel would take about 110, an estimate from its run with more fills, against about 103.8 for before at full clock: of the changed kernel's time at a clock of 0.969, some 1.2 us go when the clock is kept up, and a gap of about 6 us is there at full clock too. Both hang on late loads, and the shares can't be added, since the clock hides waits behind it.

**The baseline.** "What lies between is not in this trace, so I leave it in both kernels": it was half clock in before, which the changed kernel had in every execution and before in about half. On before at full clock the forecast's own +1.8 would have been about 105.6.

**The deferred work, +0.55.** In the profiles without a hole behind hid the last sec ends 74.94 to 75.11 behind it, against 74.12: 0.8 to 1.0. In the changed kernel's own profile the same difference less its hole is 0.94. Of the right kind, somewhat larger.

**The hole, +0.8.** In the changed kernel L541 did not wait, which the prediction had named as a sign that it is wrong: k_val of batch 1 came at 36.54, right behind num. VectorE's row turns began 0.58 ahead of hid (31.23) and its product of 1280 elements took 1.47, not 2.2, so that it ended 4.6 us behind hid's start instead of 5.9; TensorE's hid and num took 4.7. In the run with before's loads L541 did wait, 0.75, but for a quarter of v that landed late, while the product had ended at 29.86. The size was right there by luck.

**"From 40 us on ... I see no second place of the kind"** failed: st_bn of chunk 1 stands ahead of zT and waited for rows that come by DRAM, which cost TensorE 1.29 in the changed kernel's profile. Runs with st_bn at the same place show it in some profiles and not in others.

**The faster rival** missed its sign by 0.3 (w_ch1's half was there at 3.79, and 3.5 was set), though its mechanism came in part: from 4 to 6 us the engines moved 314 GB/s instead of 192. It gained nothing: k_dir stood at 10.07 as before, and k_cp waited anyway, as the prediction said.

**What stays open:** why the landings differ between executions, which moves the time with before's order of loads by 2.6 us at a like clock (106.0 at 0.978, 108.7 at 0.984) and head pairs in before by 6. The last kernel's time at full clock (1.026 of before) is not a matter of the loads alone: its hid lies 1.3 behind the 25.1 of that one execution, and the two waits shown are for steps on VectorE that these edits had put ahead of others. What an order that moves the loads and no such step would take was not run.
